# Three sigmoids in one visit, sign passes behind the high half of x, and six more fills, in an mLSTM with two feed-forward layers

## The chip, the cores and the metric

The kernel runs on one core of a Trainium2 chip. The metric is the time of one execution on the device in microseconds (us); lower is better. The engines run side by side, each through its own queue in order, and wait for one another through semaphores: TensorE (PE) multiplies matrices, VectorE (DVE) and GpSimd (POOL) work element by element, ScalarE (ACT) applies functions, and SyncE (SP) issues the transfers.

## The reference

Three stages follow one another. The first is a gated recurrence over 768 steps for 2 batches and 8 heads of width 40; the other two are feed-forward layers over its 1536 tokens of width 320.

```
C = f_stab * C + i_stab * outer(v_t, k_t)
n = f_stab * n + i_stab * k_t
y_t = sigmoid(o_gate_t) * (C @ q_t) / max(|n . q_t|, 1)
...
h = x @ w_in;  x = (h - tanh(h)) @ w_out
h = x @ w_in;  out = (h * tanh(softplus(h))) @ w_out
```

## The kernel before

The recurrence is computed by chunks of 128 steps, as attention: 12 parts (6 chunks by 2 batches), numbered `j`. Each part needs masks `nb` (L342), their exponential `Dm` (L345, ScalarE; zeroed above the diagonal by GpSimd, L347), scores `sc` (L363) times `Dm` (L367, VectorE), the product `it` with the running state C (L374, L379), the product `pv` with v (L385, L389), a denominator (L394 to L396), the gate and the division into `xo` (L398, L399), and a copy of the last 64 columns (L402, ScalarE). Then TensorE transposes three tiles (`xt`, L284), ScalarE rounds them into the high half of x (L286) and VectorE takes the low half (L289). `st` (L408, L418) updates the state C.

The output gates are turned into sigmoids by `sigmoid_o` (L260), one chunk of both batches a call. `session` (L694) issues a run of calls; a sigmoid and the exponential need different tables on ScalarE, so a visit costs a table load in front, and at its end a load for the exponential with a dummy exponential (L700). Each call stands behind the instruction that the list `behind` gives it.

The tokens come in six blocks of two parts each. Layer 1 has 16 weight parts of 128 hidden units; block 0 runs its parts 0 to 7 first, two parts a step (`tile1`, steps `i` = 0 to 3), the other blocks parts 0 to 9, and the rest later. A step multiplies x with the parts (`h`, L545), then does tanh twice and a square (L567 to L569, ScalarE), two products (L572, L573, VectorE), a relu (L574), a predicated copy (L576, VectorE), the rounding into `gh` (L556, ScalarE; kept as `rounded[i]`) and the low half `gl` (L557, GpSimd). The second matmuls L608 to L610 add into `acc`.

The weights arrive as 64-bit floats and are converted part by part in `conv_w`: a shift (L198, VectorE), a sign pass (L206, ScalarE, with a Prelu), a merge (L210, VectorE), the rounding to the high half (L213, ScalarE) and the low half (L216, L217, VectorE). `head` names what the sign pass must stand behind; `first` what the shift must stand behind. From part 8 on `head` is `rems`, the newest copy of L402.

`spin` (L646) issues matmuls on constants, called fills below, to a scratch bank. `keep(n, x)` places n of them behind an instruction; for the first three steps the counts per part stand in a tuple at L551. The order on each engine is otherwise chosen by a scheduler when the kernel is built, from the dependencies and from `after`, which places an instruction behind a given one.

Of the kernel before, what the change touches and what calls it, by code (L numbers as in the profile page):

```python
# [25 lines left out]
def kernel(  # L26
# [31 lines left out]
    NP = 2  # L58
# [69 lines left out]

    texp, tbl, dls, squared = [], [], [], []

    scored, gated, rounded, relus, rems = {}, {}, {}, {}, []

    spq, cvd, hold = [], [], []

# [6 lines left out]
    def after(x):  # L141
        e = ExitStack()
        for i in x:
            e.enter_context(tc.issue_after(i.ins))
        return e
# [39 lines left out]
    def conv_w(layer, f, first=(), behind=()):  # L185
        r = raw.pop((layer, f)).rearrange("p (n t) -> p n t", t=2)
        lo32, z = r[:, :, 0], r[:, :, 1]
        zf = z.bitcast(F32)
        w = wp.tile([P, WT], F32R, tag="w", name="w")
        wf = w.bitcast(F32)  # L190

        head = texp if (layer, f) == (0, 0) else squared if layer == 0 and f < CUT[0] else rems
        if layer == 0 and f:
            head = head + [scaled[0, f - 1]]
        with after(first):
            nc.vector.tensor_scalar(lo32, in0=lo32, scalar1=29, scalar2=None, op0=ALU.logical_shift_right)  # L198
        if second:
            nc.vector.scalar_tensor_tensor(  # L200
                lo32, in0=z, scalar=0x80000000, in1=lo32, op0=ALU.bitwise_and, op1=ALU.bitwise_or
            )
            scaled[layer, f] = nc.scalar.activation(out=zf, in_=zf, func=AF.Copy, scale=2.0 ** -111)
        else:
            with after(head):
                scaled[layer, f] = nc.scalar.activation(  # L206
                    out=zf, in_=zf, func=AF.Prelu, scale=2.0 ** -111, alpha=-2.0 ** 32
                )
        with after(behind):
            third[layer, f] = nc.vector.scalar_tensor_tensor(  # L210
                z, in0=z, scalar=3, in1=lo32, op0=ALU.logical_shift_left, op1=ALU.bitwise_or
            )
        cvd[:] = [nc.scalar.activation(out=w[:, 0:WC], in_=zf, func=AF.Copy)]  # L213
        eng = nc.gpsimd if (layer, f) == (0, 0) else nc.vector
        with after(scored[NP + 1] if (layer, f) == (0, CUT[0] - 1) else []):
            eng.tensor_tensor(w[:, WC:WT], in0=zf[:, 0:REM0], in1=wf[:, 0:REM0], op=ALU.subtract)  # L216
        lows[layer, f] = eng.tensor_tensor(w[64:P, REM0:REM1], in0=zf[64:P, REM0:REM1], in1=wf[64:P, REM0:REM1], op=ALU.subtract)  # L217
        wtile[layer, f] = w
# [46 lines left out]
    def at_ps(shape, name):  # L265
        p, tag = at_pools[0]
        if len(at_pools) > 1:
            at_pools.append(at_pools.pop(0))
        return p.tile(shape, F32, tag=tag, name=name)
# [29 lines left out]
    def keep(n, x):  # L299
        if fill:  # L300
            fill[0](n, [x])

    def attention(j):
# [67 lines left out]
        if c > 0:  # L371
            it = at_ps([P, HG, 2, D1], "it")
            for g in range(HG):
                nc.tensor.matmul(  # L374
                    it[:, g].rearrange("p h d -> p (h d)"), lhsT=q[:, g, :],
                    rhs=C[:, g].rearrange("p h d -> p (h d)"), start=True, stop=True,
                )
            u = uT[:, c, hs].rearrange("p (r g o) -> p r g o", r=2, o=1)
            nc.vector.tensor_tensor(  # L379
                hv.rearrange("p (r g) d -> p r g d", r=2), in0=it.rearrange("p g r d -> p r g d"),  # L380
                in1=u.to_broadcast([P, 2, HG, D1]), op=ALU.mult,
            )
        pv = at_ps([P, H, D1], "pv")
        for h in range(H):
            x = nc.tensor.matmul(pv[:, h, :], lhsT=Dm[:, h, :], rhs=v[:, h, :], start=True, stop=True)  # L385
# [13 lines left out]
        gated[j] = nc.vector.scalar_tensor_tensor(  # L399
            x, in0=x, scalar=1 / WS, in1=den.to_broadcast([P, H, D]), op0=ALU.mult, op1=ALU.mult  # L400
        )
        rems[:] = [nc.scalar.activation(out=xo[:, j, DM:3 * P], in_=xo[:, j, 2 * P:DM], func=AF.Copy)]  # L402
        yield "x"
        if c + 1 < NCH:
            st = at_ps([P, HG, D1], "st")
# [128 lines left out]
    def mm1(i):  # L534
        l, bi, fs, nt = span(i)
        t = ps_h.tile([P, MX], F32, tag="h", name="h")[:, 0:len(fs) * nt]
        xh, xl = xT[l, bi]
        pairs = [
            (HI0, xh, 0), (HI1, xh, 1), (HI0, xl, 0), (HI1, xl, 1), (LO0, xh, 0), (LO1, xh, 1), (PCH, xh, 2), (PCH, xl, 2),
        ]  # L540
        for k, f in enumerate(fs):
            w = wtile[l, f]
            for n, (o, x, kk) in enumerate(pairs):
                with after([] if n else hold):
                    y = nc.tensor.matmul(  # L545
                        t[:, k * nt:(k + 1) * nt], lhsT=w[:, o:o + P], rhs=x[:, kk, :], start=(n == 0),
                        stop=(n == len(pairs) - 1),
                    )
            hold[:] = [y] if i < CUT[0] // NP - 1 else []
            if i < 3:  # L550
                keep((3, 8, 5, 5, 2, 2)[f], y)  # L551
        hps[i] = t

    def split_g(i, g, n):
# [87 lines left out]
    def program():  # L642
# [183 lines left out]
        for i in range(len(tiles)):  # L826
# [29 lines left out]
            if l == 0:  # L856
                tile1(i)
                if 1 < i < 4:
                    session(2 * i - 3, 2 * i - 1 + (i > 2), i == 3, [cvd[0], relus[2]] if i < 3 else [rounded[2], relus[3], rounded[3]])
                qm.append(i)  # L860
                if len(qm) > LAG:
                    mm2(qm.pop(0))
# [77 lines left out]
```

## Time and profile before

| | |
|---|---|
| median of 3 runs | 458.38 us (457.74 to 458.99) |
| profiled execution | 460.05 us, of which the span from first to last instruction is 458.0 |
| TensorE busy | 443.5 us, 97% |
| VectorE, ScalarE, GpSimd busy | 303.0, 284.2, 103.8 us |
| mean granted TensorE clock | 0.989 |

The profile is one execution. Starts and lengths are microseconds from the start of the span. A busy TensorE is not always one at full clock; the granted clock is listed apart, 1.00 being 2.4 GHz and 0.50 being 1.2 GHz. A time in brackets is how long the engine sat idle before an instruction, with the instruction that ended the wait.

### The profile page before, as it was taken

How to read it: one execution, taken by the hardware profiler on the slowest of the kernel's cores; microseconds unless marked ns; L12 is line 12 of the kernel's file. 1: busy time of each engine (PE TensorE's matmuls, PEld its weight loads, DVE VectorE, ACT ScalarE, POOL GpSimd, SP SyncE). 2: the span in 40 equal slices, each digit the busy share in tenths (PEclk: the TensorE clock that was granted, in tenths of full speed). 3: DMA queues.
4: the chain of work that ended last, by engine and by line, in shares of the span. 5: the costliest groups of instructions: out<-in, count | busy, mean ns of one | idle time of the engine just before them, and what ended most of it. 6: DMA issues, size and time to landing. Idle time of an engine off the chain costs nothing.

```text
span 458.0 us, 7957 instructions
## 1 busy us (share of the span) xinstructions
PE 443.5 (97%) x3100; PEld 404.2 (88%) x3100; DVE 303.0 (66%) x524; ACT 284.2 (62%) x519; POOL 103.8 (23%) x119
## 2 busy tenths in 40 slices
PE   9889998899999999899999999999999999999997
PEld 5647987799999999799999999999899899988996
DVE  7899769958798889356899986989622212221112
ACT  6688697577585685698889877676533333332331
POOL 2306334435255323143333332000000000000000
PEclk9989999989999999899999999999999999999999
DMA  8985525322342321001112210345010000010001
GB/s 258 374 293 173 175 63 172 111 72 82 95 153 58 100 73 55 1 1 64 56 50 75 74 66 1 104 150 186 4 39 19 1 0 2 6 53 0 1 0 57
DMA packets 22728, 38.03 MB, mean 83 GB/s; under 512 B 1348, under 2 KB 17028, under 8 KB 22692
## 3 DMA queue, kind: packets, MB, share of 16 engines
q1 hardware_dynamic: 22692, 37.54, 25.3%
q8 instruction: 24, 0.39, 0.3%
q14 instruction: 12, 0.10, 0.1%
HBM read 35.41 MB, written 1.97 MB: 82 GB/s over the span
## 4 chain that ended last, share of the span: by engine, by line
PE 59%; DVE 3%; ACT 1%; issue 0%; ACTq 0%
PE h L545 30%; PE acc L608 9%; PE acc L610 9%; PE acc L609 9%; PE xt L284 1%; DVE g L576 1%; ACT raw L206 0%; DVE Dm L367 0%; DVE w L217 0%; DVE den L395 0%; ACT u L574 0%; DVE xo L399 0%; DVE hv L379 0%; DVE hv L389 0%; DVE xo L398 0%
## 5 line engine op out<-in xcount | busy, mean ns | idle before, releaser
L545 PE MATMUL h<-xT,w 128*128 128x256 f32 (+1 forms) x1152 | 207.0, 323 | 4.0 <-ACT xT L286 2.1
L545 PEld LDWEIGHTS h<-xT,w 128*128 128x128 f32 x1152 | 169.6, 191 | 20.9 <-ACT xT L286 2.4
L608 PE MATMUL acc<-w,gh 128*128 128x320 f32 x384 | 119.8, 313 | 1.4 <-ACT gh L556 1.4
L609 PE MATMUL acc<-w,gh 128*128 128x320 f32 x384 | 118.9, 311 | 0.0
L610 PE MATMUL acc<-w,gl 128*128 128x320 f32 x384 | 115.4, 313 | 0.5 <-POOL gl L557 0.5
L557 POOL TENSOR_TENSOR gl<-g,gh 128x512 fp32r<-128x512 f32 x48 | 63.8, 1331 | 132.6 <-ACT gh L556 132.5
L589 DVE TENSOR_TENSOR gl<-g,gh 128x512 fp32r<-128x512 f32 x48 | 33.1, 690 | 88.0 <-ACT g L588 87.9
L608 PEld LDWEIGHTS acc<-w,gh 128*128 128x128 f32 x384 | 72.5, 189 | 3.8 <-ACT gh L556 1.6
L587 ACT ACTIVATE gh<-h 128x512 fp32r<-128x512 f32 x48 | 28.7, 597 | 75.3 <-PE h L545 75.1
L609 PEld LDWEIGHTS acc<-w,gh 128*128 128x128 f32 x384 | 72.5, 189 | 2.5
L610 PEld LDWEIGHTS acc<-w,gl 128*128 128x128 f32 x384 | 70.6, 189 | 1.6 <-POOL gl L557 0.8
L556 ACT ACTIVATE gh<-g 128x512 fp32r<-128x512 f32 x48 | 30.3, 631 | 26.7 <-DVE g L576 24.9
L576 DVE COPY_PREDICATED g<-u,t 128x512 f32<-128x512 uint32 x48 | 40.4, 845 | 7.8 <-ACT u L574 7.4
L572 DVE TENSOR_TENSOR g<-u,h 128x512 f32<-128x512 f32 x48 | 32.5, 678 | 16.4 <-ACT u L569 8.9
L574 ACT ACTIVATE u<-u,bias 128x512 f32<-128x512 f32 x48 | 34.9, 728 | 6.4 <-DVE g L572 6.4
L213 ACT ACTIVATE w<-raw 128x704 fp32r<-128x704 f32 x32 | 27.5, 863 | 13.6 <-DVE raw L210 13.3
L210 DVE SCALAR_TENSOR_TENSOR raw<-raw 128x704 uint32<-128x704 uint32 x32 | 32.1, 1013 | 1.7 <-ACT raw L206 1.1
L573 DVE TENSOR_TENSOR t<-h,t 128x512 f32<-128x512 f32 x48 | 32.7, 681 | 0.0
L567 ACT ACTIVATE u<-h 128x512 f32<-128x512 f32 x48 | 28.3, 590 | 5.2 <-PE h L545 4.9
L216 DVE TENSOR_TENSOR w<-raw,w 128x576 fp32r<-128x576 f32 x31 | 27.8, 896 | 5.6 <-ACT w L213 5.5
L569 ACT ACTIVATE u<-u 128x512 f32<-128x512 f32 x48 | 30.7, 639 | 0.0
L568 ACT ACTIVATE t<-h 128x512 f32<-128x512 f32 x48 | 28.6, 596 | 0.0
(104 smaller groups left out, 449.8 us busy)
## 6 DMA issues: line engine op xcount, KB each, us to landing
raw<-in_w_dram SPq DMA_DIRECT2D x32, 704.0 KB
qk_t<-in_qk_dram SPq DMA_DIRECT2D x12, 512.0 KB
kv_t<-in_kv_dram SPq DMA_DIRECT2D x12, 324.0 KB
out_dram<-xo SPq DMA_DIRECT2D x12, 160.0 KB
xo<-in_og_dram SPq DMA_DIRECT2D x2, 800.0 KB
xo<-in_og_dram SPq DMA_DIRECT2D x1, 320.0 KB
sd<-nr SPq DMA_DIRECT2D x20, 4.0 KB
md<-nr SPq DMA_DIRECT2D x10, 8.0 KB
```

Of the source, the lines that this page charges most:

```text
L210: third[layer, f] = nc.vector.scalar_tensor_tensor(z, in0=z, scalar=3, in1=lo32, op0=ALU.logical_shift_left, op1=ALU.bitwise_or)
L545: y = nc.tensor.matmul(t[:, k * nt:(k + 1) * nt], lhsT=w[:, o:o + P], rhs=x[:, kk, :], start=(n == 0), stop=(n == len(pairs) - 1),)
L557: nc.gpsimd.tensor_tensor(gl, in0=g, in1=gh.bitcast(F32), op=ALU.subtract)
L569: squared[:] = [nc.scalar.activation(out=u, in_=u, func=AF.Square, scale=G_SA)]
L572: mark[:] = [nc.vector.tensor_tensor(g, in0=u, in1=h, op=ALU.mult)]
L573: nc.vector.tensor_tensor(t, in0=h, in1=t, op=ALU.subtract)
L574: relus[i] = nc.scalar.activation(out=u, in_=u, func=AF.Relu, bias=bias[:, 0:1])
L576: nc.vector.copy_predicated(out=g, mask=u.bitcast(U32), data=t)
L589: mark.append(nc.vector.tensor_tensor(gl, in0=g, in1=gh.bitcast(F32), op=ALU.subtract))
L608: turn(lambda: nc.tensor.matmul(a, lhsT=gh[:, sl], rhs=wh, start=(f in ends_), stop=False))
L609: turn(lambda: nc.tensor.matmul(a, lhsT=gh[:, sl], rhs=wl, start=False, stop=False))
L610: turn(lambda: nc.tensor.matmul(a, lhsT=gl[:, sl], rhs=wh, start=False, stop=end))
```

## The change

Five edits. The tuple of fills has 14 instead of 8 behind part 1 of step 0. The sigmoids of chunks 3 to 5 all stand behind the third rounding (`rounded[2]`), where only that of chunk 3 did. The list `rems` is gone: from part 8 on a sign pass stands behind the high half of x that was last made (`chain[1]`), except for parts 8 and 9, whose sign pass is bound to nothing. The shifts of parts 8 and 9 stand behind the first `hv` product and the gate product of part `j` = 2 alone, and no longer behind step 3's. The copy of L402 goes through a helper and has L159 in rows of the change. Four lines were added, so rows of the change have line numbers up to 4 higher: L571 to L573 are the tanh passes and the square, L576 and L577 the products, L578 the relu, L580 the predicated copy, L560 the rounding, L704 the dummy and its load.

```diff
@@ conv_w
-        head = texp if (layer, f) == (0, 0) else squared if layer == 0 and f < CUT[0] else rems
+        head = texp if (layer, f) == (0, 0) else squared if layer == 0 and f < CUT[0] else [] if (layer, f) in slots else chain[1:2]
...
-        with after(first):
+        with after(slots.get((layer, f), first)):
             nc.vector.tensor_scalar(lo32, in0=lo32, scalar1=29, scalar2=None, op0=ALU.logical_shift_right)
@@ attention
-            nc.vector.tensor_tensor(
+            y = nc.vector.tensor_tensor(
                 hv.rearrange("p (r g) d -> p r g d", r=2), in0=it.rearrange("p g r d -> p r g d"),
                 in1=u.to_broadcast([P, 2, HG, D1]), op=ALU.mult,
             )
+            if j == NP:
+                slots[0, CUT[0]] = [y]
...
-        rems[:] = [nc.scalar.activation(out=xo[:, j, DM:3 * P], in_=xo[:, j, 2 * P:DM], func=AF.Copy)]
+        if j == NP:
+            slots[0, CUT[0] + 1] = [gated[j]]
+        copy_r(0, xo[:, j, DM:3 * P], xo[:, j, 2 * P:DM])
@@ mm1
-                keep((3, 8, 5, 5, 2, 2)[f], y)
+                keep((3, 14, 5, 5, 2, 2)[f], y)
@@ program
-                    session(2 * i - 3, 2 * i - 1 + (i > 2), i == 3, [cvd[0], relus[2]] if i < 3 else [rounded[2], relus[3], rounded[3]])
+                    session(2 * i - 3, 2 * i - 1 + (i > 2), i == 3, [cvd[0], relus[2]] if i < 3 else [rounded[2]] * 3)
```

ScalarE at the end of block 0, before: from the third rounding (L556) to the sign passes of parts 8 to 10. `xo` is the output gate and later x, `scr` the dummy's target, `xT` the high half of x.

```order
L556 ACTIVATE gh<-g 128x512
L260 ACTIVATE xo<-xo 128x2x320
L402 ACTIVATE xo<-xo 128x64
...
L574 ACTIVATE u<-u,bias 128x512
L260 ACTIVATE xo<-xo 128x2x320
L286 ACTIVATE xT<-xt 128x3x128
L556 ACTIVATE gh<-g 128x512
L260 ACTIVATE xo<-xo 128x2x320
L700 ACT_TABLE_LOAD
L700 ACTIVATE scr<-bias 128x1
L345 ACTIVATE Dm<-nb 128x512
L206 ACTIVATE raw<-raw 128x704 x3
```

The same place in the change.

```order
L560 ACTIVATE gh<-g 128x512
L260 ACTIVATE xo<-xo 128x2x320 x3
L704 ACT_TABLE_LOAD
L704 ACTIVATE scr<-bias 128x1
L159 ACTIVATE xo<-xo 128x64
...
L578 ACTIVATE u<-u,bias 128x512
L286 ACTIVATE xT<-xt 128x3x128
L560 ACTIVATE gh<-g 128x512
L206 ACTIVATE raw<-raw 128x704 x3
L345 ACTIVATE Dm<-nb 128x512 x2
```

The last two sigmoids, the load and the dummy moved ahead of the copy of `xo`, and the sign passes ahead of the first exponential.

VectorE in the third step of block 0, before: `hv` is the product with the state, g the result of the step.

```order
L576 COPY_PREDICATED g<-u,t 128x512
L217 TENSOR_TENSOR w<-raw,w 64x128
L367 TENSOR_TENSOR Dm<-sc,Dm 128x512 x2
L216 TENSOR_TENSOR w<-raw,w 128x576
L379 TENSOR_TENSOR hv<-it,uT 128x328
L389 TENSOR_TENSOR hv<-hv,pv 128x328
```

The same place in the change.

```order
L577 TENSOR_TENSOR t<-h,t 128x512
L367 TENSOR_TENSOR Dm<-sc,Dm 128x512
L217 TENSOR_TENSOR w<-raw,w 64x128
L367 TENSOR_TENSOR Dm<-sc,Dm 128x512
L216 TENSOR_TENSOR w<-raw,w 128x576
L379 TENSOR_TENSOR hv<-it,uT 128x328
L580 COPY_PREDICATED g<-u,t 128x512
L391 TENSOR_TENSOR hv<-hv,pv 128x328
```

The predicated copy, which the third rounding waits for, moved behind the scores' products and the first `hv` product.

ScalarE at the end of the last attention parts, before, from the square of a step (L569) on.

```order
L569 ACTIVATE u<-u 128x512
L402 ACTIVATE xo<-xo 128x64
L206 ACTIVATE raw<-raw 128x704 x3
L286 ACTIVATE xT<-xt 128x3x128
L574 ACTIVATE u<-u,bias 128x512
L286 ACTIVATE xT<-xt 128x3x128
L556 ACTIVATE gh<-g 128x512
```

The same place in the change.

```order
L573 ACTIVATE u<-u 128x512
L159 ACTIVATE xo<-xo 128x64
L286 ACTIVATE xT<-xt 128x3x128
L578 ACTIVATE u<-u,bias 128x512
L286 ACTIVATE xT<-xt 128x3x128
L206 ACTIVATE raw<-raw 128x704 x2
L560 ACTIVATE gh<-g 128x512
L206 ACTIVATE raw<-raw 128x704
```

The three sign passes moved behind both high halves of x, the third of them behind the rounding as well.

## Rows read from the trace of the kernel before

**Rows 1.** The page: busy us of each engine, granted clock in 40 slices.

```profile
PE 443.5 (97%) x3100; PEld 404.2 (88%) x3100; DVE 303.0 (66%) x524; ACT 284.2 (62%) x519; POOL 103.8 (23%) x119
...
PEclk9989999989999999899999999999999999999999
```

**Rows 2.** Waits of TensorE, whole span: us in total, times, longest.

```profile
PE h L545 <- ACT xT L286: 2.1, 1, 2.1
...
PE acc L608 <- ACT gh L556: 1.4, 1, 1.4
...
PE sc L363 <- DVE Dm L367: 1.2, 1, 1.2
...
PE st L408 <- DVE xT L289: 0.7, 1, 0.7
PE sc L363 <- ACT Dm L345: 0.5, 1, 0.5
PE acc L610 <- POOL gl L557: 0.5, 1, 0.5
```

**Rows 3.** Windows: busy us of PE, PEld, DVE, ACT, POOL; granted clock; DMA.

```profile
30.00:35.00 5.00, 5.00 (x21) 2.62 (x21) 4.88 (x9) 3.53 (x6) 1.07 (x1) 0.68 0.87 311
...
80.00:90.00 10.00, 8.63 (x64) 8.17 (x62) 9.96 (x20) 6.39 (x12) 4.79 (x5) 1.00 0.43 127
90.00:100.00 10.00, 9.49 (x83) 8.64 (x83) 5.81 (x15) 5.78 (x14) 3.02 (x4) 0.83 0.23 67
...
180.00:200.00 20.00, 17.86 (x127) 17.52 (x126) 10.40 (x21) 15.90 (x33) 3.87 (x3) 0.91 0.00 1
```

**Rows 4.** Timeline of TensorE from 25 to 33: start, length, idle before.

```profile
25.04 1.91 PE L649 MATMUL w_ps<-const-bfloat16-1.0 128*32 128x512 bf16 x8
...
28.76 0.73 PE L545 MATMUL h<-xT,w 128*128 128x256 f32 x4 [1.56 <-ACT w L213]
...
30.85 2.32 PE L649 MATMUL w_ps<-const-bfloat16-1.0 128*32 128x512 bf16 x5
```

**Rows 5.** Timeline of ScalarE, first visit for sigmoids.

```profile
47.54 1.28 ACT L260 ACT_TABLE_LOAD   x1
48.84 1.36 ACT L260 ACTIVATE xo<-xo 128x640 f32<-128x640 f32 x2
...
50.63 0.72 ACT L260 ACTIVATE xo<-xo 128x640 f32<-128x640 f32 x1
53.94 0.26 ACT L402 ACTIVATE xo<-xo 128x64 f32<-128x64 f32 x1 [2.60 <-DVE xo L399]
55.03 0.60 ACT L567 ACTIVATE u<-h 128x512 f32<-128x512 f32 x1 [0.83 <-PE h L545]
```

**Rows 6.** Timeline of ScalarE, second visit and the sign passes behind it.

```profile
58.02 0.72 ACT L260 ACTIVATE xo<-xo 128x640 f32<-128x640 f32 x1
...
60.42 0.72 ACT L260 ACTIVATE xo<-xo 128x640 f32<-128x640 f32 x1
61.15 1.28 ACT L700 ACT_TABLE_LOAD   x1
...
63.04 2.38 ACT L206 ACTIVATE raw<-raw 128x704 f32<-128x704 f32 x3
```

**Rows 7.** Timeline of VectorE in block 1.

```profile
68.10 0.76 DVE L216 TENSOR_TENSOR w<-raw,w 128x576 fp32r<-128x576 f32 x1 [2.49 <-ACT w L213]
...
85.08 1.62 DVE L398 TENSOR_TENSOR xo<-hv,xo 128x320 f32<-128x320 f32 x1
...
88.38 0.47 DVE L398 TENSOR_TENSOR xo<-hv,xo 128x320 f32<-128x320 f32 x1
```

**Rows 8.** Timelines of ScalarE and TensorE behind the last attention parts.

```profile
182.17 2.28 ACT L206 ACTIVATE raw<-raw 128x704 f32<-128x704 f32 x3
...
185.34 0.46 ACT L286 ACTIVATE xT<-xt 128x384 fp32r<-128x384 f32 x1
...
185.85 5.94 PE L545 MATMUL h<-xT,w 128*128 128x256 f32 x34 [2.14 <-ACT xT L286]
```

More of the change, by code (lines that the diff above doesn't have):

```diff
@@ L129 @@
     texp, tbl, dls, squared = [], [], [], []
-    scored, gated, rounded, relus, rems = {}, {}, {}, {}, []
+    scored, gated, rounded, relus, slots = {}, {}, {}, {}, {}
     spq, cvd, hold = [], [], []
```

## The prediction

> **What bounds the kernel now.** I read the page's busy times and slices first. TensorE is busy 97% of the span, and its granted clock is below full in only a few slices [rows 1]. So time can come from three things alone: TensorE's waits, stretches at the lower clock (1.2 instead of 2.4 GHz), and fills that hide a wait. The waits of TensorE come next: the reader sees single pieces, each named once, and the largest is 2.1 us for the high halves of x [rows 2]. The windows then place the lower clock [rows 3]. A window's loss is its length times what is missing from 1.00: 5 x 0.32 = 1.6 us at 30 to 35, 10 x 0.17 = 1.7 at 90 to 100, 20 x 0.09 = 1.8 at 180 to 200. Each fall follows waits that stand close together: 1.56 us at 28.76 [rows 4], 1.4 and 0.5 before 91 [rows 2], 2.14 before 185.85 [rows 8]. The waits of 0.5 and 1.2 for scores, and the 0.7 for `st`, were followed by no fall. Between the first and the second fall two engines feed TensorE: VectorE is busy 9.96 of 10 us at 80 to 90 [rows 3], and ScalarE carries sigmoids, table loads and sign passes that nobody on TensorE needs at once [rows 5, 6].
>
> **The change, part by part.**
>
> *Six more fills* (14 behind part 1 of the first token tile instead of 8). Eight took 1.91 us, so 0.24 each and 1.4 for six. They start where TensorE now waits 1.56 us for the rounded weights of part 2 (L213), so they cost nothing: that wait covers them. Without the cover they would cost 1.4. What they do is keep TensorE active there. The five fills at 30.85 took 2.32 us at half clock; at 0.24 they take 1.2, and part 3's matmuls behind them, now at about 33.2, come some 1.5 us earlier, if the slowed matmuls ahead of the fills are counted too [rows 4]. That alone is no gain at the end, because VectorE is busy 4.88 of 5 us in this stretch [rows 3] and its work is not less. What passes on is settled at the end of the first token block, next.
>
> *One visit of all last sigmoids.* The order shows ScalarE doing three sigmoids, the table load and the dummy exponential right behind the third rounding (L556), where it did one sigmoid at 50.63 and then sat idle 2.60 us until the remainder copy L402 at 53.94 [rows 5]. From the end of that one sigmoid (51.3), two more at 0.72, a load of 1.28 and about 0.1 for the dummy (an estimate: between a load's end at 62.43 and the sign passes at 63.04 stand the dummy and an exponential [rows 6]) end at 54.1. The copy is 0.2 late, nothing more. The tanh pass behind it (L567) waited 0.83 for TensorE until 55.03 [rows 5]. Its matmuls now come earlier, so it starts near 54.2: 0.8 gained. The sigmoid at 58.02 no longer stands in front of the second high x, another 0.6 to 0.7 for that pass [rows 6]. VectorE's second low x sits behind the gate work of the same tile, which moves only with L567. I take 0.9 us for the start of block 1 on TensorE. Bounds: 0, if VectorE's copy_predicated (L576), which the order puts behind the first `hv` product, delays the third rounding by as much; 1.6, if the whole clock gain of the fills arrives. Term: **-0.9**.
>
> A rule speaks against this visit. The row shows a table load of 1.28 us with the first sigmoid right behind the load; no pause is in the timeline [rows 5]. The Trainium skill, page "ScalarE: Activation LUTs", section "What ACT_TABLE_LOAD costs", adds a drain of about 1380 ns to each switch, 2.66 us in all. By it the copy would come at 55.5 and the sum would be 1.4 us worse. The trace does not agree, so the row's 1.28 stands; the sum does not use the page's figure.
>
> *What leaves the start of block 1.* ScalarE had a sigmoid, a load of 1.28 and the dummy from 60.42, then an exponential, then three sign passes of 2.38 together, ending at 65.4 [rows 6]. Now the three sign passes follow L556 directly and stand ahead of the exponentials: 60.4 - 0.9 + 2.3 = 61.8, so 3.6 us earlier. VectorE waited 2.49 for the rounded weights behind them [rows 7]; that wait goes. So the scores' products come earlier, and TensorE's 0.5 (for exponentials) and 1.2 (for the scores' products) go [rows 2]. Bounds 0.5 and 1.7; with 3.6 to spare I take the upper end: **-1.7**. The freed shifts of parts 8 and 9 move by one pair of state updates only, ahead of the last C sums; the wait of 2.49 behind them is for ScalarE and already counted, so they bring nothing more. Were a load of parts 8 or 9 late, their place would cost what it is late.
>
> *The waits at 87 to 91 and the clock behind them.* VectorE has no slack at 80 to 90 [rows 3], and TensorE waits 1.4 and 0.5 for roundings that end its chain [rows 2]. VectorE enters this stretch about 3.6 earlier, TensorE 0.9 + 1.7 = 2.6 earlier. So 1.0 of the 1.9 goes, and 0.9 stays: **-1.0** (bounds 0 and 1.9). A rest of 0.9 is near the 0.7 that brought no fall, so the clock's loss of 1.7 there goes: **-1.7** (bounds 0 and 1.7).
>
> *A new wait.* At the end of block 0 TensorE arrives earlier, but L402 does not (54.1). Behind the two transposes the order has only `st`, the high-x matmuls and the masks: nothing fills. TensorE will wait for the two copies and for x in pieces, some 2 to 3 us instead of 0.7. That is the size that halved the clock in three places. The waiting is already in the 0.9; a fall would cost about 1.6, of which a part hides in the 0.9 that stays at 89. I take **+1.3** (bounds 0 and 1.6).
>
> *Sign passes behind high x.* In the last attention block three sign passes, 2.28 us, ran ahead of both high-x passes, and TensorE waited 2.14 until 185.85 [rows 8]. Its transposes had ended at 183.71. Now the order puts both high-x passes first: the second takes 0.46 behind the transposes, about 184.3, and the wait is 0.6: **-1.5** (bounds 1.3 and 1.9). A wait of 0.6 brought no fall elsewhere, so the 1.8 of the window at 180 to 200 goes: **-1.6** (bounds 0 and 1.8). The sign passes themselves are needed much later; the rounding they delay has no reader for six microseconds of matmuls (5.94 at 185.85 [rows 8]). From here on TensorE has no wait of size, so a shift passes through to the end.
>
> Sum: -0.9 - 1.7 - 1.0 - 1.7 + 1.3 - 1.5 - 1.6 = -7.1 us. The profiled execution took 460.05, so 452.95; the median of the runs is 458.38, 1.67 lower, which makes **451.3**.
>
> **Rivals.** *No fall at the end of block 0, and VectorE's margin holds in full*: 1.3 + 0.9 more, 449.1. For it: 0.5 and 1.2 in a row brought no fall before. Against it: the pieces add up to more.
>
> *VectorE stays the bound through block 1.* Some of its operations stretch: the gate product (L398) took 1.62 us at 85.08 and 0.47 at 88.38 [rows 7], in a window where GpSimd is busy 4.79 of 10 us [rows 3] (that the one causes the other is a guess). If the new order stretches more of them, the waits at 89 and the clock's loss stay: 7.1 - 1.0 - 1.7 = 4.4, and 0.7 less of the score waits gives 3.7, so 454.7.
>
> *Slower: the third rounding comes late.* L576 now stands behind the `hv` product, which waits for `it` on TensorE, which waits for the scores' products. Each microsecond by which its end passes 50.6 moves the three sigmoids, the load, L402 and both transposes by the same. At 7 us late the whole gain is gone; at 9 the kernel is slower, about 460.2. For it: the visit leaves no slack at all in front of L402 (54.1 against 53.94). Against it: VectorE's queue up to there holds the same work less one operation.
>
> *It does little*: the clock falls in all the old places and TensorE only swaps waits, 457.5.
>
> **How the numbers follow.** My forecast 0.50 (own range 449.8 to 453.0), better 0.18, VectorE bound 0.20, little 0.05, slower 0.07. The predicted time is the forecast's. No change is within 0.3%, 1.4 us. Faster holds the first three, 0.88. The range runs from below the better case (all upper bounds: 1.6 + 1.7 + 1.9 + 1.7 + 1.9 + 1.8 = 10.6 less, 447.8) to beyond the VectorE case with the first term at 0, the new fall at 1.6 and the score waits 0.5 worse (454.7 + 0.9 + 0.3 + 0.5 = 456.4); it leaves out the little and the slower case, 0.12.
>
> **What would show it.** Granted clock 1.00 at 30 to 35 and no wait before part 2: the fills. L402 near 54 behind a table load, no sigmoid later than 54: the visit. Sign passes done by 62 and no TensorE wait for scores near 70: the start of block 1. At the last attention block's end a wait under 1 us and full clock behind it. A low clock near 58 to 62 shows the new wait. Wrong it would be if L556 of the third tile starts well behind 50.6, or if TensorE shows waits in the blocks from 100 to 180 that are not there now.

## The result and the profile after

The changed kernel takes 451.42 us, median of 6 runs (451.11 to 452.11), the kernel before 458.38 in 6 runs beside them (455.80 to 460.17). The ratio is 0.9853, 95% interval 0.9824 to 0.9882. The forecast was 451.3. The profiled execution took 451.4, span 449.4, so 8.6 less than the profiled span of before.

The page after, to be held against [rows 1]: busy time of TensorE, and granted clock in 40 slices.

```profile
PE 440.0 (98%) x3106; PEld 401.1 (89%) x3106; DVE 303.9 (68%) x524; ACT 283.7 (63%) x519; POOL 106.0 (24%) x119
...
PEclk9999999999999999999999999999999999999999
```

All three low stretches are gone. The waits of TensorE after, against [rows 2]:

```profile
PE xt L284 <- DVE xo L401: 1.6, 2, 1.3
PE st L412 <- DVE xT L289: 1.4, 1, 1.4
...
PE h L549 <- ACT xT L286: 0.6, 1, 0.6
PE xt L284 <- PE st L412: 0.3, 1, 0.3
PE nb L342 <- DVE xT L289: 0.3, 1, 0.3
...
PE h L549 <- ACT w L213: 0.2, 1, 0.2
```

In this list, which shows waits of 0.2 us and more, none for scores (`sc`) is left and none for a rounding (`acc`). The wait for high x fell from 2.1 to 0.6; that for part 2's weights (L213) from 1.6 to 0.2. New is `st` with 1.4 where it had 0.7. The second of the two waits in the first row is 0.36 us at 88.30: it is all that is left of the 1.4 and 0.5 near 89.

The windows after, against [rows 3]; the granted clock is the third number from the end of a row, behind the five busy times.

```profile
30.00:35.00 5.00, 5.00 (x27) 3.09 (x28) 4.88 (x9) 3.87 (x8) 0.15 (x1) 1.00 0.91 318
80.00:90.00 10.00, 9.54 (x93) 8.62 (x92) 9.20 (x22) 5.34 (x12) 4.99 (x5) 1.00 0.31 86
90.00:100.00 10.00, 10.00 (x82) 9.32 (x83) 6.49 (x12) 8.99 (x18) 4.53 (x8) 1.00 0.37 111
180.00:200.00 20.00, 20.00 (x158) 20.00 (x157) 11.57 (x19) 17.75 (x35) 6.50 (x5) 1.00 0.01 2
```

TensorE's timeline after, at the fills, at the end of block 0 and behind the last attention block, against [rows 4, 8]:

```profile
25.20 3.22 PE L653 MATMUL w_ps<-const-bfloat16-1.0 128*32 128x512 bf16 x14
...
28.91 0.73 PE L549 MATMUL h<-xT,w 128*128 128x256 f32 x4 [0.24 <-ACT w L213]
...
30.65 1.26 PE L653 MATMUL w_ps<-const-bfloat16-1.0 128*32 128x512 bf16 x5
...
57.90 0.51 PE L412 MATMUL st<-wv,kv_t 128*40 128x41 f32 x16 [1.37 <-DVE xT L289]
...
60.20 3.43 PE L549 MATMUL h<-xT,w 128*128 128x256 f32 x28
...
178.80 4.45 PE L549 MATMUL h<-xT,w 128*128 128x256 f32 x35 [0.58 <-ACT xT L286]
```

Part 2 starts at 28.91, where it started at 28.76: the wait is filled, not shortened. The five fills behind it take 1.26 instead of 2.32 us.

ScalarE's timeline after, through the one visit, against [rows 5, 6]:

```profile
50.35 0.63 ACT L560 ACTIVATE gh<-g 128x512 fp32r<-128x512 f32 x1 [0.41 <-DVE g L580]
50.88 1.98 ACT L260 ACTIVATE xo<-xo 128x640 f32<-128x640 f32 x3
52.87 1.28 ACT L704 ACT_TABLE_LOAD   x1
...
54.27 0.24 ACT L159 ACTIVATE xo<-xo 128x64 f32<-128x64 f32 x1
54.42 0.58 ACT L571 ACTIVATE u<-h 128x512 f32<-128x512 f32 x1
...
59.84 2.32 ACT L206 ACTIVATE raw<-raw 128x704 f32<-128x704 f32 x3
```

The copy comes at 54.27 (it was 53.94), tanh at 54.42 (it was 55.03), and the sign passes end at 62.2 (they ended at 65.4). VectorE's wait of 2.49 for the rounded weights behind them is down to 0.36, and ends 3.2 earlier (68.10 before):

```profile
64.89 0.76 DVE L216 TENSOR_TENSOR w<-raw,w 128x576 fp32r<-128x576 f32 x1 [0.36 <-ACT w L213]
```

Four marks say how much earlier the program then is. The long run of `h` of block 1 starts at 60.20 (60.78 before), the seventh `h` of block 2 at 92.36 (98.16), the last attention block's transposes end at 178.22 (183.71), and the first `acc` behind that block's `h` comes at 183.09 (191.63). So 0.6, 5.8, 5.5 and 8.5 us, and 8.6 at the end: all but the first 0.6 is won at 60 to 92 and at 178 to 192. Of the 3.0 at the last place 1.6 are the shorter wait, and the rest is the clock: the 34 matmuls behind the wait took 5.94 before, and 35 take 4.45 now.

### The profile page after: what moved, and what is told of

Read it like the earlier page. It is cut to its first block, busy times and chain, and to the rows that moved or that the text cites. A ratio compares the mean times of both kernels' runs of the same rounds, so it can differ in the third digit from the quotient of the medians.

```text
span 449.4 us, 7973 instructions
## 1 busy us (share of the span) xinstructions
PE 440.0 (98%) x3106; PEld 401.1 (89%) x3106; DVE 303.9 (68%) x524; ACT 283.7 (63%) x519; POOL 106.0 (24%) x119
## 4 chain that ended last, share of the span: by engine, by line
PE 89%; DVE 7%; ACT 3%; issue 1%; DVEq 0%
PE h L549 39%; PE acc L612 12%; PE acc L614 12%; PE acc L613 12%; PE sc L363 3%; PE pv L387 3%; PE w_ps L653 2%; PE it L374 2%; PE xt L284 2%; PE nb L342 1%; DVE g L580 1%; DVE Dm L367 1%; ACT raw L206 1%; DVE t L577 1%; DVE w L216 1%
## 5 line engine op out<-in xcount | busy, mean ns | idle before, releaser
L549 PE MATMUL h<-xT,w 128*128 128x256 f32 (+1 forms) x1152 | 204.8, 321 | 1.1 <-ACT xT L286 0.6
L549 PEld LDWEIGHTS h<-xT,w 128*128 128x128 f32 x1152 | 167.6, 188 | 17.6 <-ACT xT L286 1.1
L614 PE MATMUL acc<-w,gl 128*128 128x320 f32 x384 | 113.9, 311 | 0.0
L576 DVE TENSOR_TENSOR g<-u,h 128x512 f32<-128x512 f32 x48 | 32.6, 679 | 19.6 <-ACT u L573 7.3
L560 ACT ACTIVATE gh<-g 128x512 fp32r<-128x512 f32 x48 | 30.4, 633 | 24.1 <-DVE g L580 20.6
L580 DVE COPY_PREDICATED g<-u,t 128x512 f32<-128x512 uint32 x48 | 39.8, 839 | 4.9 <-ACT u L578 4.5
L578 ACT ACTIVATE u<-u,bias 128x512 f32<-128x512 f32 x48 | 35.1, 731 | 5.2 <-DVE g L576 5.2
L577 DVE TENSOR_TENSOR t<-h,t 128x512 f32<-128x512 f32 x48 | 32.7, 682 | 0.0
L213 ACT ACTIVATE w<-raw 128x704 fp32r<-128x704 f32 x32 | 27.3, 864 | 7.1 <-DVE raw L210 6.9
L216 DVE TENSOR_TENSOR w<-raw,w 128x576 fp32r<-128x576 f32 x31 | 29.1, 938 | 3.0 <-ACT w L213 2.7
L573 ACT ACTIVATE u<-u 128x512 f32<-128x512 f32 x48 | 30.7, 643 | 0.0
L571 ACT ACTIVATE u<-h 128x512 f32<-128x512 f32 x48 | 28.5, 593 | 2.7 <-PE h L549 2.4
(104 smaller groups left out, 451.3 us busy)
```

The source lines that it names most:

```text
L549: y = nc.tensor.matmul(t[:, k * nt:(k + 1) * nt], lhsT=w[:, o:o + P], rhs=x[:, kk, :], start=(n == 0), stop=(n == len(pairs) - 1),)
L576: mark[:] = [nc.vector.tensor_tensor(g, in0=u, in1=h, op=ALU.mult)]
L577: nc.vector.tensor_tensor(t, in0=h, in1=t, op=ALU.subtract)
L578: relus[i] = nc.scalar.activation(out=u, in_=u, func=AF.Relu, bias=bias[:, 0:1])
L580: nc.vector.copy_predicated(out=g, mask=u.bitcast(U32), data=t)
L614: turn(lambda: nc.tensor.matmul(a, lhsT=gl[:, sl], rhs=wh, start=False, stop=end))
```

## The experiments

Twelve kernels were run. The ratio of each is to runs of the kernel before on the same chip. Three make one edit of the change in the kernel before, two more follow up the third of these, three undo one edit in the changed kernel, and four add something to it. The runs of before on the four chips have medians of 458.0 to 459.9, so "more than the changed kernel" below is a difference of medians from two chips. Below some 1.4 us (0.3%) it is not told from no change, and where the ratios say otherwise that is noted.

The freed shifts of parts 8 and 9 need no run: built without them, the changed kernel has the same instructions in the same order with the same waits on every engine, so this edit did nothing. The same holds for the sign passes of these parts, which are bound to nothing: bound to the high half of x like the others, they come out in the same order. Three edits are left.

**The fills alone.**

```diff
-                keep((3, 8, 5, 5, 2, 2)[f], y)
+                keep((3, 14, 5, 5, 2, 2)[f], y)
```

> The kernel before with 14 fills instead of 8 behind part 1 of the first token tile, and nothing else. My theory (the three edits are separate pieces, and VectorE and ScalarE, not TensorE, set the start of block 1): the low clock at 30 to 35 us goes (0.68 to about 1.00), the 28 matmuls of part 2 and 3 start 1 to 1.5 us earlier, but the second visit of sigmoids and the table load still stand in front of the high half of x and of the sign passes, so the waits for scores (0.5 and 1.2 us), the wait near 89 and the low clock at 90 to 100 stay. About 0.5 us faster at the end, 457.9 against 458.4, within 0.3%. Rival (the loss of clock is what is paid, wherever it falls): 1.6 us faster, 456.8. Second rival (the fills alone carry the start of block 1, the visit adds little): 4 us faster, 454.4.

Measured 457.28 (455.21 to 458.71), ratio 0.9982 [0.9959, 1.0004]: 0.7 less by the medians, where the theory had 0.5, and not told from no change. In its profile the long run of `h` in block 1 starts 1.6 us earlier than in the profile of before (60.78), and the first copy of `xo` 0.7 earlier (53.94):

```profile
59.18 2.50 PE L545 MATMUL h<-xT,w 128*128 128x256 f32 x20
```

```profile
53.24 0.26 ACT L402 ACTIVATE xo<-xo 128x64 f32<-128x64 f32 x1 [2.22 <-DVE xo L399]
```

The profile shows something else too. At the last attention block TensorE waits as long as before, and the window behind has full clock:

```profile
183.04 4.44 PE L545 MATMUL h<-xT,w 128*128 128x256 f32 x34 [2.17 <-ACT xT L286]
```

```profile
180.00:200.00 20.00, 17.83 (x140) 17.50 (x139) 10.11 (x16) 16.87 (x34) 5.43 (x5) 1.00 0.00 1
```

So a wait of this size at this place is not always followed by a fall, as the prediction had taken from one profile.

**The visit alone.**

```diff
-                    session(2 * i - 3, 2 * i - 1 + (i > 2), i == 3, [cvd[0], relus[2]] if i < 3 else [rounded[2], relus[3], rounded[3]])
+                    session(2 * i - 3, 2 * i - 1 + (i > 2), i == 3, [cvd[0], relus[2]] if i < 3 else [rounded[2]] * 3)
```

> The kernel before with the last three sigmoids all behind the third rounding, and nothing else (8 fills, old order of the sign passes). My theory: the sign passes of parts 8 to 10 end some 3 us earlier than at 65.4 us, VectorE's wait of 2.49 us near 68 goes, TensorE shows no wait for scores near 70, the waits near 87 to 91 shrink from 1.9 to under 1 us and the clock at 90 to 100 is full: 0.4 + 1.7 + 1.0 + 1.7 = 4.8 us less, 453.6 against 458.4. The wait of 2.14 us at the last attention block's end and the low clock behind it stay. Rival (the visit has no slack without the fills: the copy ahead of the transposes comes late): 1 to 2 us less, 456.4 to 457.4. Rival (the visit brings nothing, the sign passes do): within 0.3%.

Measured 452.43 (451.48 to 452.91), ratio 0.9874 [0.9845, 0.9903]. The visit by itself brings 5.6 of the 7 us (4.4 to 7.1 by the interval). Its waits of TensorE:

```profile
PE xt L284 <- DVE xo L399: 1.6, 2, 1.3
PE h L545 <- ACT w L213: 1.6, 1, 1.6
PE h L545 <- ACT xT L286: 1.2, 1, 1.2
```

The waits for scores and roundings are gone, as the theory had it. But the wait for high x in the last attention block is 1.2 already, not 2.1, though no sign pass was unbound there: with ScalarE's work moved, the scheduler put one of the three sign passes ahead of a tanh square (L569), earlier.

```profile
175.95 0.84 ACT L206 ACTIVATE raw<-raw 128x704 f32<-128x704 f32 x1
176.69 0.62 ACT L569 ACTIVATE u<-u 128x512 f32<-128x512 f32 x1
177.21 1.57 ACT L206 ACTIVATE raw<-raw 128x704 f32<-128x704 f32 x2
```

That was in no expectation. It may account for the 1.2 us more than the theory's 453.6, though these lie inside the interval. At the start of block 1, on the other hand, this profile shows nothing won:

```profile
61.20 3.43 PE L545 MATMUL h<-xT,w 128*128 128x256 f32 x28
```

This is 0.4 later than in the profile of before (60.78), at nearly the same low clock at 30 to 35 us (0.66 and 0.68).

**The sign passes alone.**

```diff
-        head = texp if (layer, f) == (0, 0) else squared if layer == 0 and f < CUT[0] else rems
+        head = texp if (layer, f) == (0, 0) else squared if layer == 0 and f < CUT[0] else rems if (layer, f) in ((0, CUT[0]), (0, CUT[0] + 1)) else chain[1:2]
```

> The kernel before with the sign passes from part 10 on behind the high half of x instead of behind the copy of the last 64 columns, and nothing else. My theory: at the end of the last attention block TensorE's wait falls from 2.14 us to about 0.6, and the granted clock of the 20 us behind it rises from 0.91 to full: 1.5 + 1.6 = 3.1 us less, 455.3 against 458.4; the start of block 1 stays as it was. Rival (only the wait counts, the clock falls all the same): 1.5 us less, 456.9. Rival (the sign passes are late for their own readers, and another wait takes its place): within 0.3%.

Measured 462.78 (462.34 to 464.70), ratio 1.0109 [1.0078, 1.0140]: slower, which no theory had. Its largest wait of TensorE, and the window in which it lies:

```profile
PE h L545 <- DVE t L573: 4.3, 5, 1.3
...
PE acc L610 <- POOL gl L557: 1.5, 4, 0.5
```

```profile
200.00:300.00 100.00, 94.61 (x662) 89.78 (x661) 71.27 (x132) 75.19 (x135) 28.89 (x21) 1.00 0.15 50
```

The changed kernel has neither wait; the same window of it is full:

```profile
200.00:300.00 100.00, 100.00 (x702) 96.81 (x701) 87.71 (x147) 81.25 (x144) 26.81 (x20) 1.00 0.22 72
```

That is 5.4 us of TensorE lost, 3.6 of it between 225 and 260 (31.41 of 35 busy). Where the two known kernels mix `h` and `acc` finely in the late parts of layer 1, here the order came out in whole groups, 32 `h` and then 24 `acc`, and the next `h` waits for VectorE's product `t`. What the edit won earlier was paid back, and more, by another order far behind it.

**The same, at one place.** The edit was therefore narrowed to the three sign passes in the last attention block; this leaves VectorE's and GpSimd's orders as they were, and those of the late parts too.

```diff
-        head = texp if (layer, f) == (0, 0) else squared if layer == 0 and f < CUT[0] else rems
+        head = texp if (layer, f) == (0, 0) else squared if layer == 0 and f < CUT[0] else chain[1:2] if layer and f < 3 else rems
```

> The kernel before with one triple of sign passes alone, that of the first three parts of layer 2, behind the high half of x; all the others stay behind the copy of the last 64 columns. The first run of this piece moved every sign pass from part 10 on, and the order of layer 1's late matmuls came out in whole groups (32 h, then 24 acc), with 4.3 us of waits for VectorE between 225 and 260 us that neither kernel has; here that stretch keeps the order of before. My theory (the move is worth the wait, and the clock behind the wait falls in a part of the executions only, since a wait of 2.17 us was followed by full clock in the run with the fills alone): the wait falls from 2.14 to about 0.6 us, and the median is 1.5 to 2.5 us below that of before. Rival (the prediction's term in full, -3.1 us): 3 us or more below. Rival (another wait takes its place): within 0.3% of before.

Measured 456.10 (454.29 to 457.06), ratio 0.9952 [0.9930, 0.9975], so 2.2 us less (1.1 to 3.2 by the interval), in the theory's range; the rival's 3.1 is at the interval's end. The row shows the wait at 0.58:

```profile
183.44 4.45 PE L545 MATMUL h<-xT,w 128*128 128x256 f32 x35 [0.58 <-ACT xT L286]
```

**Fills in the wait of the last attention block**, in the kernel before (`more[0]` is `spin`, kept from block 0).

```diff
+        if (layer, bi, pos) == (0, NB - 1, 1):
+            more[0](8, [x])
```

> The kernel before with eight fills behind the last transpose of the last attention block, where TensorE waits 2.14 us for the high half of x; the sign passes stay where they were, so the wait itself is not shortened, only filled (8 x 0.24 = 1.9 us). It tells apart the two terms of the sign passes' move. My theory (a wait of this size halves the granted clock behind it, and a filled one does not): the matmuls behind the wait start at the same time as before, and the clock at 180 to 200 us is full instead of 0.91: 1.6 to 1.8 us less, 456.7 against 458.4. Rival (the clock there has nothing to do with the wait): the clock falls all the same, within 0.3% of 458.4. Rival (fills behind a transpose come late and push the matmuls back): 1 to 2 us more.

Measured 465.00 (464.53 to 465.70), ratio 1.0156 [1.0124, 1.0187]. It doesn't answer: the late parts came out in groups again, with 2.8 us of waits for `t` and 1.5 for `gl`, and the order around the fills changed as well.

**The change with 8 fills.**

```diff
-                keep((3, 14, 5, 5, 2, 2)[f], y)
+                keep((3, 8, 5, 5, 2, 2)[f], y)
```

> The changed kernel with 8 fills instead of 14 behind part 1 of the first token tile. My theory: the low clock at 30 to 35 us is back (about 0.7), the third rounding begins about 0.5 us later, and everything behind it moves by that: 0.5 to 0.9 us more than the changed kernel's 451.4, so 451.9 to 452.3; no wait for scores comes back. Rival (the visit leaves no slack at all, so the loss of the fills costs in full): 1.6 us more, 453.0, or with a new low clock near 58 to 62 us 454.5. Rival (VectorE hides it): 451.4.

Measured 451.81 (451.62 to 452.46), ratio 0.9848 [0.9813, 0.9883]: 0.4 more than the changed kernel by the medians, nothing by the ratios (0.9848 against 0.9853). In its profile the wait of 1.56 for part 2 and the low clock are back (0.71 at 30 to 35), and the long run of `h` in block 1 starts at 60.64, 0.44 later. The wait for `st` behind the transposes is 0.72, as before, and not 1.37: the longer wait comes with the fills (it is 1.22 with the fills alone).

**The change without the visit.**

```diff
-                    session(2 * i - 3, 2 * i - 1 + (i > 2), i == 3, [cvd[0], relus[2]] if i < 3 else [rounded[2]] * 3)
+                    session(2 * i - 3, 2 * i - 1 + (i > 2), i == 3, [cvd[0], relus[2]] if i < 3 else [rounded[2], relus[3], rounded[3]])
```

> The changed kernel with the last two sigmoids back behind the third relu and the third step's rounding of before, so that the second visit with its table load stands again in front of the sign passes and the exponentials of block 1. My theory: the waits for scores near 70 us come back (1.7 us), those near 89 grow to about 1.9, the clock there falls again (1.7): 4 to 5 us more than 451.4, 455.4 to 456.4. Rival (the fills and the unbound sign passes carry block 1, the visit little): under 1.5 us more, at most 452.9.

Measured 462.40 (461.46 to 463.22), ratio 1.0074 [1.0047, 1.0100]: 11 us more than the change. Here too the late parts are in groups, and TensorE is busy 94.65 of the 100 us from 200 on. Without those 5.4 us 5.6 are left, as much as the visit alone brought; the run has other differences, so this agreement is weak evidence.

**The change with the sign passes back.**

```diff
-        head = texp if (layer, f) == (0, 0) else squared if layer == 0 and f < CUT[0] else [] if (layer, f) in slots else chain[1:2]
+        head = texp if (layer, f) == (0, 0) else squared if layer == 0 and f < CUT[0] else [] if (layer, f) in slots else rems
```

> The changed kernel with the sign passes from part 10 on back behind the copy of the last 64 columns, so ahead of the high half of x in the last attention block. My theory: the wait there is 2.1 us instead of 0.58 and the granted clock of the 20 us behind it falls to about 0.91: 3.1 us more than 451.4, 454.5. Rival (the clock does not fall): 1.5 us more, 452.9. Rival (block 1 has freed so much that ScalarE is early here too): 451.4.

Measured 452.29 (451.25 to 455.23), ratio 0.9863 [0.9825, 0.9901]. This is, instruction for instruction, the kernel before with fills and visit alone. So the sign passes are worth 0.9 us in the changed kernel by the medians, 0.5 by the ratios, neither told from no change, and not 3.1. The row says why. The wait they shorten is 1.23 there, not 2.14, and the window behind it has full clock:

```profile
179.98 4.45 PE L549 MATMUL h<-xT,w 128*128 128x256 f32 x34 [1.23 <-ACT xT L286]
```

```profile
55.00:65.00 10.00, 7.87 (x73) 6.83 (x68) 8.81 (x15) 8.13 (x15) 3.56 (x3) 0.83 0.23 67
180.00:200.00 20.00, 20.00 (x157) 19.93 (x158) 11.11 (x18) 16.71 (x33) 6.47 (x5) 1.00 0.00 1
```

Its first window shows the new fall near 58 to 62 that the prediction had priced at 1.3: 10 x 0.17 = 1.7 us of clock. Yet its last transposes end at about 178.75, only 0.5 later than in the changed kernel. One of its six executions ran at a mean clock of 0.985 and took 455.23; where its clock fell is not recorded.

**Two more table loads** in the changed kernel.

```diff
+                if c0 == 3:
+                    for g in (AF.Sigmoid, AF.Exp):
+                        with after(tbl):
+                            tbl[:] = [nc.scalar.activation(out=scr, in_=bias[:, 0:1], func=g)]
```

> The changed kernel with two more table loads (a dummy sigmoid and a dummy exponential on one column) at the end of the single visit: 2 x 1.28 us and two dummies of about 0.2, some 2.8 us of ScalarE in front of the copy of the last 64 columns. It asks what a microsecond in front of that copy costs. My theory (no slack ahead of the copy, and TensorE is full from there on): the copy moves from 54.27 to 57.1 us, the first matmuls of block 1 start 2.8 us later, and 2 to 2.8 us arrive at the end; with the clock falling in a wait near 57 to 62 us that is now 4 to 5 us long, up to 1.6 more: 453.4 to 455.8 against 451.4. Rival (VectorE is the bound of block 1, ScalarE has slack): under 0.7 us more, at most 452.1. Rival (a table load costs more than its own length, some 1.4 us each, as the Trainium skill's page ScalarE: Activation LUTs has it in What ACT_TABLE_LOAD costs): the copy at 59.9 us.

Measured 455.26 (454.98 to 455.83), ratio 0.9922 [0.9893, 0.9951]: 3.8 more than the changed kernel (3.2 by the ratios). ScalarE's timeline, the transpose that waits for the copy, and the window that follows:

```profile
54.30 1.28 ACT L708 ACT_TABLE_LOAD   x1
55.59 0.20 ACT L708 ACTIVATE scr<-bias 128x1 f32<-128x1 f32 x1
55.81 1.28 ACT L708 ACT_TABLE_LOAD   x1
57.10 0.20 ACT L708 ACTIVATE scr<-bias 128x1 f32<-128x1 f32 x1
57.21 0.24 ACT L159 ACTIVATE xo<-xo 128x64 f32<-128x64 f32 x1
```

```profile
57.51 0.33 PE L284 MATMUL xt<-ident,xo 128*128 128x128 f32 x1 [2.82 <-ACT xo L159]
```

```profile
60.00:70.00 10.00, 9.16 (x63) 8.85 (x63) 8.40 (x15) 7.72 (x14) 3.58 (x3) 0.66 0.18 57
```

The copy comes 2.94 later (57.21 against 54.27), which is two loads of 1.28, two dummies and little else: in these rows a load is over when its row ends. TensorE waits 2.82 for the copy, so there is no slack ahead of it, as the prediction had it for its slower rival. The profiled execution ends 4.4 later than that of the changed kernel (span 453.8 against 449.4). The later copy and the low clock, which costs 3.4 us at 60 to 70 (10 x 0.34), make 6.3, so 1.9 of them are hidden; the run cannot part the two.

**20 fills** in the changed kernel.

```diff
-                keep((3, 14, 5, 5, 2, 2)[f], y)
+                keep((3, 20, 5, 5, 2, 2)[f], y)
```

> The changed kernel with 20 fills instead of 14 behind part 1 of the first token tile. With 14 TensorE waits only 0.24 us more there, so the cover is used up. My theory: part 2 starts 1.2 us later (6 x 0.24 less the 0.24), and VectorE, busy 4.9 of 5 us there, is not early enough to hide it: 0.5 to 1.2 us more than 451.4 at the end, 451.9 to 452.6. Rival (VectorE sets the stretch, TensorE's lateness is hidden): 451.4, within 0.1%. Rival (TensorE is the only bound from here on): 1.2 us more or above, 452.6.

Measured 452.50 (451.76 to 452.75), ratio 0.9861 [0.9829, 0.9893]: 1.1 more, the theory's size (0.4 by the ratios). The length of the fills is not what the profile shows of it. Part 2 starts 0.55 later (29.46), and the five fills behind part 2 no later than in the changed kernel (30.60 against 30.65). The long run of `h` in block 1 starts 0.58 later and takes 4.64 instead of 3.43 us, for here the clock falls at 55 to 65 (0.83):

```profile
60.78 4.64 PE L549 MATMUL h<-xT,w 128*128 128x256 f32 x28
```

The span is 1.2 longer (450.6 against 449.4). So about half of it is there when block 1 starts, and the rest comes with the fall.

**Fills in the new wait.** First two and six of them, behind both pairs of transposes of block 1.

```diff
+        if layer == 0 and bi == 1:
+            keep((2, 6)[pos], x)
```

> The changed kernel with fills in the waits that the visit left at the end of block 0: two behind the first transposes and six behind the second (8 x 0.24 = 1.9 us, where TensorE waits 0.35, 1.37 and 0.32 us). My theory: the waits end with ScalarE's copies, so filling them brings no time by itself, and the clock there is full in the changed kernel's profile already: 451.4, within 0.3%, with the granted clock at 1.00 in every run. Rival (the clock falls there in some executions, as in the runs with a mean clock of 0.995, and that costs): 0.3 to 1 us less. Rival (fills behind transposes push the state update and the masks back): 0.5 to 1.5 us more.

Measured 459.53 (458.75 to 461.43), ratio 1.0012 [0.9989, 1.0035]: 8 us more than the changed kernel, at a clock of 0.999 to 1.000 in all 12 executions. The late parts are in groups once more (4.3 us for `t`, 1.3 for `gl`). Then five behind the second pair alone, `keep((0, 5)[pos], x)`, which leaves the other order as it is.

> The changed kernel with five fills (5 x 0.24 = 1.2 us) behind the second pair of transposes at the end of block 0, where TensorE waits 1.37 us for the low half of x; the order of everything else, ScalarE's and the late matmuls of layer 1 too, stays that of the changed kernel. The first run of this kind (eight fills) came out with the late matmuls in whole groups and 4.3 us of waits for VectorE there, so it did not answer the question. My theory (the wait ends with the copy and the low half, and the filled wait only keeps the clock up): 451.4 within 0.3%, with a mean clock of 1.00 where the changed kernel had 0.995 to 0.996 in half its executions, worth at most 0.5 us: 450.9 to 451.6. Rival (fills in the wait push the state update back): 0.5 us or more above.

Measured 451.06 (450.76 to 451.58), ratio 0.9846 [0.9817, 0.9876], with a mean clock of 1.000 in five of its six executions. TensorE's timeline shows the wait filled:

```profile
56.55 1.26 PE L655 MATMUL w_ps<-const-bfloat16-1.0 128*32 128x512 bf16 x5
57.99 0.51 PE L414 MATMUL st<-wv,kv_t 128*40 128x41 f32 x16 [0.18 <-DVE xT L291]
```

It has the lowest median of all kernels run. That is 0.36 below the changed kernel, inside the 0.3% that is not told from no change here.

## Why the prediction was right, and where it was not

The total was right, and most steps showed in the rows. But that it came out within 0.1 us was in part luck. The terms were read from the profiled execution of 460.05; against the profiled execution of the changed kernel the gain is 8.65, not 7.1. The terms thus fell 1.55 short there, and the step of 1.67 to the median counted falls as a gain that most executions of before don't all have; the two cancelled. One step failed, and some terms were off in opposite directions.

*The fills*: right in the rows. The wait before part 2 is down to 0.24, the clock is full, and the fills behind it take 1.26 for the 1.2 forecast. What they are worth at the end is not told from no change: put into the kernel before they bring 0.7, taken out of the change they cost 0.4 by the medians and nothing by the ratios.

*The start of block 1 (-0.9)*: 0.6 in the profile, but not as worked out. The prediction had the visit win there. With the fills alone the long run of `h` starts at 59.18 and the first copy of `xo` comes at 53.24; with the visit as well they are at 60.20 and 54.27. So, by one profile each, the fills win 1.6, and 1.0 of it is gone in the change. Of this the visit takes 0.45: the copy comes 3.92 behind the start of the third rounding instead of 3.47, with two more sigmoids and the load ahead of it. The other 0.6 is there already when the third rounding starts (50.35 against 49.77), from a cause that was not traced.

*What the visit does behind that*: the steps came as worked out (copy 54.27 for 54.1, tanh 54.42 for 54.2, sign passes done at 62.2 for 61.8, no wait for scores). Of the 1.9 us near 89 the prediction left 0.9; 0.36 is there. And it did not see that the visit alone also nearly halves the last wait. Measured alone the visit brings 5.6 us, where the terms -1.7, -1.0 and -1.7 make 4.4; the interval, 4.4 to 7.1, does not show that they are too small. On the price of a load the rows, 1.28 us with the next activation right behind, stand against the rule that the prediction cites. The Trainium skill, page "ScalarE: Activation LUTs", section "What ACT_TABLE_LOAD costs", adds a drain of about 1380 ns to each switch, by which, as an estimate, the copy of the run with two more loads would be 2.76 us later still; it came 2.94 later in all.

*The new fall (+1.3)*: the wait came as described, 0.35, 1.37 and 0.32 us in pieces; the fall behind it is in some profiles only, and none is in that of the changed kernel. Two have it, with 1.7 us of clock at 55 to 65 (10 x 0.17). In the run with the sign passes back the long run of `h` starts 0.2 later than in the changed kernel, and the last transpose near 89 (89.89 against 89.13) 0.8 later; with 20 fills the two are 0.6 and 1.3 (90.39). So some 0.5 to 0.7 of the 1.7 passes on.

*The sign passes (-1.5 and -1.6)*: this is the step that failed. The wait came out as forecast, 0.58. But what it was measured against, 2.14 us and a low clock, is the kernel before; behind the visit the wait is 1.21 and 1.23 in two profiles and the clock full. So 0.65 of wait is left to win there, and the medians give 0.9 (not told from no change), where the edit alone brings 2.2. The prediction added two edits as if each met the kernel before; they share a part.

*The clock terms*: the profiled execution of before had all three falls and a mean clock of 0.989. In 63 executions of it beside these runs, nine had a mean clock of 0.995 to 0.998 and a median of 456.2 us, 24 had 0.991 to 0.993 and 457.6, and 30 had 0.981 to 0.989 and 459.9. The three executions of the changed kernel with 0.995 to 0.996 took 451.2 to 452.1. At like clock the change thus brings about 4.5 us (456.2 less 451.7). With the fills alone two executions ran at 1.000 and took 455.2 and 455.9, against 451.1 to 451.5 of the changed kernel at 1.000: 4.3, much the same. By this reckoning the other 2.5 of 7 are the falls it avoids. The prediction's waits alone were -5.1, its clock terms -2.0 with the new fall; its step of 1.67 from the profiled execution to the median can be read as the falls that most executions don't all have.

*The rivals*: VectorE did not stay the bound; the third rounding began at 50.35 and was not late. The case that came nearest beside the forecast was the better one, no fall at the end of block 0, but with a smaller last term.

What stays open: why the scheduler turned to whole groups in four of the twelve kernels wasn't traced. In three of them it costs 5.4 us of TensorE between 200 and 300, in the one with fills behind the last attention block 4.0 (busy 96.02 of 100). It is not all: the sign passes moved at one place bring 2.2, moved at all places they lose 4.8 by the medians, and of the 7.0 between the two the 5.4 leave 1.6 without a cause. Waits are not the whole of it: between these two profiles TensorE is busy 443.8 and 440.9 us for the same 3100 matmuls.

## What to carry to other kernels

When several edits shorten waits of the same engine, price the later ones against the kernel with the earlier ones in it, and ask whether the first moves the work that the second is to move. Where a scheduler sets the order, compare the whole order, far behind the edit too, before a single edit is timed: here it decided between 2.2 us won and 4.8 lost for the same idea. And read from several executions what a low clock costs, since one profile may show all the falls or none. Work put into an engine's idle time can still be late for what stands behind it: here the copy came 0.45 later.

## What the runs showed of the hardware

The same wait is followed by the lower clock in one profile and by full clock in another. The wait of 1.56 to 1.60 us before part 2 stands in the profiles of six kernels with 8 fills; in four the granted clock at 30 to 35 us is 0.66 to 0.78, in two (both kernels with sign passes moved alone) it is 1.00. The wait of 2.1 us behind the last attention block was followed by 0.91 at 180 to 200 us in the kernel before and by 1.00 in the one with the fills alone.

Some of VectorE's operations stretch at the start of block 1. Two shifts of weight parts earlier, and two there, in VectorE's timeline of the changed kernel; of the latter one took 0.52 us and the other 1.63:

```profile
21.60 0.95 DVE L198 TENSOR_SCALAR raw<-raw 128x704 uint32<-128x704 uint32 x2
...
59.72 2.06 DVE L198 TENSOR_SCALAR raw<-raw 128x704 uint32<-128x704 uint32 x2
```

The gate product too takes 1.42 us at 83.30 and 0.49 at 87.66 in the same kernel. GpSimd's timeline at the two places:

```profile
60.08 1.31 POOL L561 TENSOR_TENSOR gl<-g,gh 128x512 fp32r<-128x512 f32 x1 [6.69 <-ACT gh L560]
...
83.08 1.29 POOL L561 TENSOR_TENSOR gl<-g,gh 128x512 fp32r<-128x512 f32 x1
```

The stretched shift ends at 61.78, GpSimd's operation at 61.39; the stretched gate product at 84.72, GpSimd's at 84.37. In the whole profile eight shifts and gate products are stretched, and each overlaps a GpSimd operation and ends 0.34 to 0.39 us behind it. Not every overlap stretches: a shift at 211.30 took 0.51 beside a `gl` that had started at 211.26. No run takes the GpSimd operation away, so that it is the cause, which the prediction called a guess, is likely but not shown.
